# Loading 16 of 128 partitions of two experts' second weights in transfers of 8 partitions

## The chip, the cores and the metric

The kernel runs on one core of a Trainium2 chip. Five engines work side by side: PE (matrix products), DVE (vector work), ACT (scalar functions, copies out of PSUM), POOL and SP, which here mainly issue transfers. Sixteen DMA engines move data between HBM and SBUF, the on-chip memory of 128 partitions. Time is the device time of one execution in microseconds (us); the median of several executions counts.

## What is computed

Two stages follow each other. Attention over 8 batches, 8 heads, 576 positions and head size 64, in which heads 0 to 3 see the last 32 positions and heads 4 to 7 every fourth of the last 128; then a mixture of 8 experts with 4 slots each, on 4608 rows of width 512.

```python
def _attn_ref(q, k, v):                       # (8, 8, 576, 64) each
    scores = scale * np.matmul(q, k.transpose(0, 1, 3, 2))
    ...
    return np.matmul(attn, v)

def _moe_ref(x, phi, w1, w2):                 # x: (4608, 512), w1: (8, 512, 1024), w2: (8, 1024, 512)
    logits = x @ phi
    d = softmax of logits over the rows
    slot_input = d.T @ x                      # 32 slots, 4 for each expert
    for e in range(E):
        h = np.maximum(slot_input[e] @ w1[e], 0.0)
        slot_out[e] = h @ w2[e]
    c = softmax of logits over the slots
    return c @ slot_out
```

All inputs are float32 in HBM, and the output is float32. The weights of one expert are 2 MB (w1) and 2 MB (w2) there.

## The kernel before

**Loads.** All inputs but the first q and k come through POOL's queue, which is issued in the order in which the program is written. A load converts from float32 to float16 on its way, so a weight matrix of 2 MB becomes 1 MB in SBUF: 128 partitions with 4096 values each. Partition p of w2 holds the 8 rows 8p to 8p + 7 of the matrix side by side, which lie one after the other in HBM as well.

**Homes.** SBUF has eight large buffers, `home0` to `home7`. Batch b's raw q, k and v go to `homes[b]` (`load_batch`, L161). When the batch has been used up, expert b's weights take their place: w1 in the first half (`load_w1`, L237), w2 in the second (`load_w2`, L253). `load_w1(e)` and, for experts 0 to 4, `load_w2(e)` are issued within the attention loop (L638 to L641) after the work of batch e; w1 of expert 7 and w2 of experts 5, 6 and 7 follow the loop (L645 to L648). The w2 of expert 6 is loaded in a first half and two quarters, the w2 of expert 7 by left and right half of the columns and each half in two pieces, so that the left half of the result can be finished before the right one.

**Waits of the loads.** Loads on POOL's queue use eight semaphores in turn, so a load also waits until the one eight places ahead of it has landed. A load into a home waits in addition for the last reader of what was there.

**Order of the work.** In the attention loop over 32 units (two heads of one batch each) PE, ACT and DVE follow an order that a scheduler made. From L650 on ("tail") the order is written out by hand. There the slots' inputs are completed (`siT`, L689), then `expert_in(pr)` multiplies them by the w1 of two experts (L712), `expert_turn(pr)` transposes the result into `hTp` (L726 to L731), and `expert_out(e)` multiplies by w2 and adds up all experts in the PSUM tile `sop` (L741). For experts 6 and 7 this is split into the two halves of the columns (L793 to L798): for each half the rest of expert 6, expert 7, a copy of `sop` to `so` (by ACT for the left half, by DVE for the right one), and five output tiles. `finish_tile` (L770) multiplies by the softmax weights (`f`, L782), scales on ACT and DVE in turn (`ot`, L786 and L788) and issues the store on SP's queue (L791). Seven whole tiles follow. The last pieces of w2 that are loaded are those of the right half of expert 7 (L273).

The change touches `load_w2` and adds one constant next to `NV` (L40).

Of the kernel before, what the change touches and what calls it, by code (L numbers as in the profile page):

```python
# [37 lines left out]
OUT_COLS = [sum(nj for _, nj in OUT_TILES[:i]) for i in range(len(OUT_TILES))]  # L38
NU = 4 * B
NV = 2  # L40
SIDES = ((0, DMODEL // 2), (DMODEL // 2, DMODEL))
PIECES = ((0, 6), (6, 8))
HALF = 4
# [16 lines left out]
def kernel(  # L60
# [10 lines left out]
    nc = tc.nc  # L71
# [15 lines left out]
    for n, (nm, ten, by) in enumerate((("qp", q, nc.sync), ("kp", k, nc.scalar))):  # L87
        first[nm] = stage[0:NP, 768 * n : 768 * n + 768].rearrange("p (g x) -> p g x", g=2)
        by.dma_start(
            out=first[nm],  # L90
            in_=ten[0, 0:2].rearrange("h s d -> (h s) d").rearrange("(g p r) d -> p g (r d)", g=2, r=RP),
# [3 lines left out]
    def kept(shape, name, dt=FP16):  # L95
        return keep.tile(shape, dt, name=name, tag=name)
# [24 lines left out]
    ends = kept([128, 2, 130], "ends")  # L121
    vp = [kept([128, NKB + 1, 4, D + 1], f"vp{i}") for i in range(NV)]
    vd = [kept([128, 16, D + 1], f"vd{i}") for i in range(2)]
# [9 lines left out]
    for i in range(2):  # L133
        nc.vector.memset(vd[i][:, :, D : D + 1], 1.0)
    for i in range(NV):
        nc.vector.memset(vp[i][:, :, :, D : D + 1], 1.0)
# [72 lines left out]
    def select_v(b):  # L209
        raw, last = raws[b]["vp"], raws[b]["vt"]  # L210
        for i in range(2):
            sel = ps_s.tile([128, 2, 2, 4, D], FP32, name=f"sel{b}_{i}", tag="s")
            for r in range(4):
                for n in range(2):
# [8 lines left out]
                    )  # L223
            nc.scalar.copy(out=vp[b % NV][:, 2 * i : 2 * i + 2, :, 0:D], in_=sel[:, :, 0])
        end = ring.tile([128, 2, 4, D], FP32, name=f"sel{b}_2", tag="ring")
        for r in range(4):
# [7 lines left out]
            )  # L234
        nc.scalar.copy(out=vp[b % NV][:, 4:6, :, 0:D], in_=end)

# [9 lines left out]
    def load_half(e, side):  # L246
        d0, d1 = SIDES[side]
        nc.gpsimd.dma_start(
            out=w_tiles[e][1][:, HALF:8, d0:d1],
            in_=moe_w2[e].rearrange("(p c) f -> p c f", p=128)[:, HALF:8, d0:d1],  # L250
        )

    def load_w2(e):  # L253
        w2t = w_tiles[e][1]
        w2_from = moe_w2[e].rearrange("(p c) f -> p c f", p=128)
        if e == E_EXP - 2:
            nc.gpsimd.dma_start(
                out=w2t[:, 0:HALF].rearrange("p c f -> p (c f)"),
                in_=w2_from[:, 0:HALF].rearrange("p c f -> p (c f)"),
            )  # L260
            load_half(e, 0)
            return
        if e < E_EXP - 2:
            nc.gpsimd.dma_start(
                out=w2t.rearrange("p c f -> p (c f)"), in_=w2_from.rearrange("p c f -> p (c f)")
            )
            return
        w2t = w_tiles[e][1] = w2t.rearrange("p c f -> p (c f)").rearrange("p (s c f) -> p s c f", s=2, c=8)
        for n, (d0, d1) in enumerate(SIDES):
            if n == 1:  # L270
                load_half(e - 1, 1)
            for c0, c1 in PIECES:
                nc.gpsimd.dma_start(out=w2t[:, n, c0:c1], in_=w2_from[:, c0:c1, d0:d1])  # L273
# [148 lines left out]
    def values(u):  # L422
# [11 lines left out]
        for h in range(2):  # L434
            mms = []
            for blk in range(NKB):
                if plain:
                    mms.append((blk, Pp[:, h, blk, 0:128], vp[b % NV][:, blk, hl + h, :]))
                    if blk > 0:
                        mms.append((blk, Pp[:, h, blk - 1, 128:256], vp[b % NV][:, blk - 1, hl + h, :]))  # L440
                elif blk < 4:
# [100 lines left out]
    def front_slots(b, up=None):  # L542
# [3 lines left out]
        for n in range(9):  # L546
            j = n % 4
            d0, d1 = (0, DMODEL) if n == 8 else SIDES[n // 4]
            nc.tensor.matmul(  # L549
# [15 lines left out]
    def last_slots(last, dcs):  # L565
        er, x = Er[(B - 1) % 2], xs[B - 1]
        for dc in dcs:
            to = last[:, N_SLOTS * dc : N_SLOTS * dc + N_SLOTS]
            for blk in range(4):
                for g in range(2):  # L570
                    d0, d1 = SIDES[g]
                    nc.tensor.matmul(
# [42 lines left out]
    for u in range(NU - 2):  # L615
        st = scores(u + 1)
        if u + 3 < NU:
            regroup(u + 3)
        values(u)
        softmax_parts(u + 1, st)  # L620
        if u + 3 < NU:
            transposes(u + 3)
        b, ph = divmod(u - 4, 4)
        if b >= 0:
            if ph == 1:
                front_logits(b)
            elif ph == 2:
                front_rows(b)
            elif ph == 3:
                front_slots(b)  # L630
        if u == 1:
            spread_phi()
        if u >= 1:
            x_transposes(u - 1)
        if u % 4 == 3 and u // 4 + 1 < B:
            spread_v(u // 4 + 1)
            select_v(u // 4 + 1)
        if u % 4 == 2 and u // 4 < E_EXP - 1:  # L638
            load_w1(u // 4)
            if u // 4 < E_EXP - 3:  # L640
                load_w2(u // 4)  # L641
        if 26 <= u:
            nc.gpsimd.memset(hTp[u - 26], 0.0)

    load_w1(E_EXP - 1)  # L645
    load_w2(E_EXP - 3)
    load_w2(E_EXP - 2)
    load_w2(E_EXP - 1)  # L648

# [25 lines left out]
    for c in range(2):  # L675
# [14 lines left out]
        out=siT,  # L690
# [45 lines left out]
    def expert_out(e, side=None, chs=range(8)):  # L736
        d0, d1 = (0, DMODEL) if side is None else SIDES[side]
        w2t = w_tiles[e][1][:, side] if e == E_EXP - 1 else w_tiles[e][1][:, :, d0:d1]
        for ch in chs:
            j = ch % 4  # L740
            nc.tensor.matmul(  # L741
                sop[32 * j : 32 * j + 32, d0:d1],
                hTp[e % 4][:, ch, 28 - 4 * e : 60 - 4 * e],
                w2t[:, ch, :],
                start=(e == 0 and ch < 4),
                stop=(e == E_EXP - 1 and ch >= 4),
                skip_group_check=True,
            )
# [43 lines left out]

    for n, (d0, d1) in enumerate(SIDES):  # L793
        expert_out(E_EXP - 2, n, range(HALF, 8))
# [40 lines left out]
```

## Time and profile before

| | |
|---|---|
| median of 3 runs | 181.22 us (181.01 to 181.52) |
| the profiled execution | 181.12 us |
| its span, first to last instruction | 179.4 us |
| PE, DVE, ACT, POOL busy | 145.9, 124.1, 116.2, 52.9 us |
| mean granted clock of PE | 0.902 |
| HBM read, written | 62.02 MB, 9.44 MB |
| weight loads of 1 MB (as written to SBUF) | 14, 28.0 us from issue to landing in the median |

The profile is one execution. Its page gives the busy time of each engine, the span in 40 slices, the transfers by queue, the chain of work that ended last, and the costliest groups of instructions. The trace behind it gives every instruction and every packet that the DMA engines moved, with start, length and size. A line such as "L741" is a line of the kernel as printed above; "sop<-home,hTp" reads as written tile and read tiles. Queue q0 is POOL's, q1 SP's, q10 ACT's; q8 and q14 bring instructions.

### The profile page before, as it was taken

What the parts mean: (1) busy time and instruction counts of PE and PEld (TensorE: products, weight loads), DVE (VectorE), ACT (ScalarE), POOL (GpSimd) and SP (SyncE); (2) the same over time, 40 slices, a digit from 0 to 9 for tenths busy, and PEclk for the clock granted to TensorE, in tenths of its full rate; (3) what the DMA queues carried; (4) which work ended last, traced back from release to release, by engine and by line L of the source; (5) the groups of instructions that cost most, each with busy time, mean ns of one, the idle gap of its engine ahead of it and who ended that gap; (6) DMA issues with size and microseconds to landing.
All of it is one profiled execution on the core that took longest, in us unless ns stands there. A gap on an engine that the chain in (4) does not pass through costs nothing.

```text
span 179.4 us, 5142 instructions
## 1 busy us (share of the span) xinstructions
PE 145.9 (81%) x2138; PEld 98.0 (55%) x2138; DVE 124.1 (69%) x341; ACT 116.2 (65%) x216; POOL 52.9 (30%) x86
## 2 busy tenths in 40 slices
PE   6549988999989989989998998998888997797000
PEld 2324666777576667667666757765658343342000
DVE  7407699689799978978979979876862011799200
ACT  2236768687888789789789788877721131699100
POOL 7946545454554644401110005006111100000000
PEclk9975699579999999999999999999998599999755
DMA  5999999999999999999999999999999999999995
GB/s 154 193 199 202 202 203 201 201 203 202 203 202 201 202 201 204 219 221 210 212 225 212 216 219 212 217 216 210 223 214 214 212 194 192 264 384 422 433 425 227
DMA packets 29238, 41.11 MB, mean 229 GB/s; under 512 B 1696, under 2 KB 26400, under 8 KB 26784
## 3 DMA queue, kind: packets, MB, share of 16 engines
q0 software_dynamic: 24416, 30.68, 98.0%
q1 hardware_dynamic: 4592, 9.82, 14.1%
q10 hardware_dynamic: 208, 0.29, 0.6%
q8 instruction: 16, 0.26, 0.5%
q14 instruction: 6, 0.05, 0.1%
HBM read 62.02 MB, written 9.44 MB: 398 GB/s over the span
## 4 chain that ended last, share of the span: by engine, by line
PE 30%; DMA 28%; DVE 17%; ACT 9%; issue 5%; POOL 3%; DVEq 0%; ACTq 0%; POOLq 0%
DMA home<-in_moe_w_dram 24%; PE o L448 6%; DMA home<-in_v_dram 4%; PE rgx L468 4%; ACT qT L305 4%; DVE ot L788 4%; PE sel L227 3%; PE l L486 3%; ACT pr L369 3%; PE s L343 3%; DVE x L453 3%; DVE P L395 2%; PE f L782 2%; DVE kTd L320 2%; PE u L549 2%
## 5 line engine op out<-in xcount | busy, mean ns | idle before, releaser
L453 DVE TENSOR_TENSOR x<-o,rc 128x640 f16<-128x640 f32 x32 | 26.3, 821 | 0.4
L369 ACT ACTIVATE pr<-s 128x960 f16<-128x960 f32 (+1 forms) x32 | 22.9, 761 | 1.6 <-PE s L343 1.6
L376 ACT ACTIVATE pd<-s 128x640 f16<-128x640 f32 x32 | 22.0, 713 | 2.1 <-PE s L352 2.0
L171 POOL DMA_DIRECT2D home<-in_v_dram x24 | 16.6, 692 | 14.9 <-DMA home<-in_k_dram 8.8
L448 PE MATMUL o<-vd,P 128*128 128x65 f16 x256 | 14.5, 198 | 3.2 <-DVE x L453 2.6
L240 POOL DMA_DIRECT2D home<-in_moe_w_dram x8 | 4.2, 531 | 40.8 <-PE rgq L315 33.4
L474 ACT COPY xT<-rgx 128x512 f16<-128x512 f16 x16 | 9.4, 586 | 10.2 <-PE rgx L468 10.2
L448 PEld LDWEIGHTS <-P 128*128 128x128 f16 x288 | 12.2, 100 | 6.8 <-DVE x L453 3.6
L385 DVE TENSOR_TENSOR Pp<-pr,fixed 128x1280 f16<-128x1280 f16 (+1 forms) x32 | 15.4, 497 | 0.3 <-ACT pr L369 0.3
L448 PE MATMUL o<-vp,Pp 128*128 128x65 f16 x288 | 15.3, 201 | 0.0
L468 PE MATMUL rgx<-fixed,x 128*128 128x128 f16 x155 | 14.0, 222 | 1.3 <-DVE x L453 0.6
L448 PEld LDWEIGHTS <-Pp 128*128 128x128 f16 x288 | 12.0, 102 | 4.1 <-issue 2.4
L788 DVE TENSOR_SCALAR ot<-f,rrow 128x256 f32<-128x256 f32 (+1 forms) x24 | 12.8, 610 | 2.1 <-PE f L782 2.1
L305 ACT COPY qT<-rgq 128x576 f16<-128x576 f16 x16 | 10.2, 639 | 6.1 <-PE rgq L304 5.4
L395 DVE TENSOR_TENSOR P<-pd,fixed 128x1024 f16<-128x1024 f16 x16 | 10.8, 672 | 4.7 <-ACT pd L376 4.7
L468 PEld LDWEIGHTS <-x 128*128 128x128 f16 x160 | 10.1, 98 | 6.6 <-issue 4.2
L786 ACT ACTIVATE ot<-f,rrow 128x256 f32<-128x256 f32 (+1 forms) x24 | 11.9, 601 | 2.5 <-PE f L782 1.7
L320 ACT COPY qT<-rgq 128x576 f16<-128x576 f16 x16 | 10.2, 640 | 4.1 <-PE rgq L315 4.0
L782 PE MATMUL f<-so,ET 128*128 128x256 f16 (+1 forms) x48 | 10.7, 324 | 2.3 <-ACT ot L786 1.1
L320 DVE COPY kTd<-rgk 128x576 f16<-128x576 f16 x16 | 12.3, 772 | 0.0
L197 POOL DMA_DIRECT2D home<-in_k_dram x15 | 10.0, 667 | 7.8 <-DMA home<-in_q_dram 7.1
L315 PEld LDWEIGHTS <-home 96*128 96x128 f16 x192 | 10.4, 103 | 3.3 <-DMA home<-in_q_dram 2.0
(119 smaller groups left out, 319.4 us busy)
## 6 DMA issues: line engine op xcount, KB each, us to landing
home<-in_moe_w_dram POOLq DMA_DIRECT2D x14, 1024.0 KB, 28.0
out_dram<-ot SPq DMA_DIRECT2D x5, 1024.0 KB, 7.8
home<-in_q_dram POOLq DMA_DIRECT2D x15, 288.0 KB, 9.8
home<-in_k_dram POOLq DMA_DIRECT2D x15, 288.0 KB, 9.9
home<-in_v_dram POOLq DMA_DIRECT2D x16, 256.0 KB, 9.8
out_dram<-ot SPq DMA_DIRECT2D x8, 256.0 KB, 2.9
out_dram<-ot SPq DMA_DIRECT2D x4, 512.0 KB, 7.2
home<-in_moe_w_dram POOLq DMA_DIRECT2D x2, 384.0 KB, 22.5
```

Of the source, the lines that this page charges most:

```text
L171: nc.gpsimd.dma_start(out=dst, in_=v[b, h0 : h0 + n_h, r0 : r0 + 4 * n_p, :].rearrange("h (p r) d -> p h (r d)", r=4),)
L305: nc.scalar.copy(out=dst[:, 0:S].rearrange("c (p r) -> c p r", r=RP), in_=rg.rearrange("c r p -> c p r"),)
L320: (nc.scalar.copy if nm == "q" else nc.vector.tensor_copy)(out=dst[:, 0:S].rearrange("c (g p a) -> c g p a", g=4, a=3), in_=rg.rearrange(" ...
L369: nc.scalar.activation(out=(pr[:, :, 0 : 3 * QW], pr[:, :, 3 * QW :])[part], in_=st[:, :, 0 : (480, 224)[part]], func=AF.Exp, scale=SCALE,)
L376: nc.scalar.activation(out=pr[:, part].rearrange("p c e t -> p e c t"), in_=st[:, :, 0 : 2 * DW].rearrange("p e (c t) -> p e c t", c=2), f ...
L385: nc.vector.tensor_tensor(out=Pp[:, :, b0 : b0 + nb, 0:w], in0=pr[:, :, b0 * QW : b0 * QW + nb * w].rearrange("p h (t c) -> p h t c", c=w) ...
L395: nc.vector.tensor_tensor(out=P1.rearrange("p a c t -> p (a c) t"), in0=pr[:, :, :, 0:128].rearrange("p a c t -> p (a c) t"), in1=mask[:, ...
L448: nc.tensor.matmul(ot[:, h, blk], lhs, rhs, start=(n == 0), stop=(n == len(mms) - 1), skip_group_check=True)
L453: nc.vector.tensor_tensor(out=xs[b][:, :, 2 * D * hp : 2 * D * hp + 2 * D].rearrange("p t (h d) -> p h t d", h=2), in0=ot[:, :, :, 0:D], i ...
L468: nc.tensor.transpose(rg[:, 128 * blk : 128 * blk + 128], x[:, blk, hl : hl + 128], ident)
L782: nc.tensor.matmul(fp, ET[:, c0 : c0 + 127 * nj + 1 : nj], so[:, d0:d1], start=True, stop=True)
L788: nc.vector.tensor_scalar(out=ot[:, j], in0=fp, scalar1=scale, scalar2=None, op0=ALU.mult)
```

## The change

The w2 of experts 1 and 4 is no longer loaded in one transfer of 128 partitions with 4096 values each, but in four: partitions 0 to 111 whole, partitions 112 to 119 whole, then of partitions 120 to 127 the first 256 values, and then their other 3840. The other experts go through the same loop with one piece, as before.

```diff
 NV = 2
+UNEVEN = ((0, 112, 0, 4096), (112, 120, 0, 4096), (120, 128, 0, 256), (120, 128, 256, 4096))
 SIDES = ((0, DMODEL // 2), (DMODEL // 2, DMODEL))
...
         if e < E_EXP - 2:
-            nc.gpsimd.dma_start(
-                out=w2t.rearrange("p c f -> p (c f)"), in_=w2_from.rearrange("p c f -> p (c f)")
-            )
+            whole = w2t.rearrange("p c f -> p (c f)"), w2_from.rearrange("p c f -> p (c f)")
+            pieces = UNEVEN if e in (1, 4) else ((0, 128, 0, 4096),)
+            for p0, p1, x0, x1 in pieces:
+                to, of = (ap[p0:p1, x0:x1] for ap in whole)
+                nc.gpsimd.dma_start(out=to, in_=of)
             return
```

POOL issues six more transfers; no other engine's instructions change, and neither do the bytes.

## The prediction

> **What bounds the kernel now.** I read the page first. Its slices and queue rows say that the transfer engines never rest and that nearly all of their time belongs to one queue, POOL's loads (q0).
>
> ```profile
> DMA  5999999999999999999999999999999999999995
> ...
> q0 software_dynamic: 24416, 30.68, 98.0%
> q1 hardware_dynamic: 4592, 9.82, 14.1%
> q10 hardware_dynamic: 208, 0.29, 0.6%
> q8 instruction: 16, 0.26, 0.5%
> ```
>
> Next the chain that ended last, between 135 and 180 us (start, length, what). The reader is to see that its longest piece is the last weight load, and that everything from 155.24 on hangs on it.
>
> ```profile
> 140.13 15.06 DMA home<-in_moe_w_dram
> ...
> 155.24 0.30 PE sop L741 x2
> ...
> 155.63 0.43 DVE so L796
> ...
> 156.11 0.83 PE f L782 x6
> ```
>
> Then the timeline of PE at that place (start, length, engine, line, count, idle time before and who ended it). PE waits for weights only twice, at 154.56 and 155.24; `sop` of the left half, at 150.89, waited for DVE's `hTp` and not for a load.
>
> ```profile
> 150.89 0.73 PE L741 MATMUL sop<-home,hTp 128*32 128x512 f16 x16 [0.27 <-DVE hTp L731]
> 152.09 2.01 PE L782 MATMUL f<-so,ET 128*128 128x256 f16 x12 [0.48 <-ACT so L796]
> 154.03 0.29 PE L741 MATMUL sop<-home,hTp 128*32 128x256 f16 x4
> 154.56 0.40 PE L741 MATMUL sop<-home,hTp 128*32 128x256 f16 x6 [0.24 <-DMA home<-in_moe_w_dram]
> 155.24 0.29 PE L741 MATMUL sop<-home,hTp 128*32 128x256 f16 x2 [0.28 <-DMA home<-in_moe_w_dram]
> ```
>
> So there is little to gain and all to lose: without any wait for weights `sop` would start at 154.03 and its 0.29 + 0.40 + 0.29 us would end at 155.01 in place of 155.53. Earlier weights are worth at most 0.5 us; later ones cost the whole delay.
>
> Last, stretches of time (length, busy time and count of PE, PEld, DVE, ACT, POOL, the granted clock, DMA share, GB/s):
>
> ```profile
> 100.00:125.00 25.00, 22.91 (x391) 16.22 (x389) 20.63 (x54) 20.51 (x37) 4.87 (x10) 1.00 1.03 216
> ...
> 152.00:152.50 0.50, 0.41 (x4) 0.38 (x4) 0.00 (x0) 0.14 (x2) 0.00 (x0) 1.00 1.15 155
> 152.50:153.00 0.50, 0.48 (x5) 0.28 (x4) 0.49 (x2) 0.50 (x2) 0.00 (x0) 1.00 1.00 135
> 153.00:154.00 1.00, 1.00 (x6) 0.47 (x5) 1.00 (x3) 1.00 (x4) 0.00 (x0) 1.00 0.79 106
> ```
>
> The rate falls from 216 to 135 GB/s before the last load has landed: some of the 16 engines have run dry while others still carry weights. The trace's packet records (start, length, bytes of each) show which. Followed from packet to packet they fall into 16 unbroken chains, one an engine; I call them lanes. In a 1 MB weight load each lane moves 8 rows of 8192 bytes, one every 606 ns, and one completion packet of 22 ns: 8 x 606 + 22 = 4870 ns, which is the step from one landing to the next (120.4, 125.3, 130.1 us). The last load's sixteen completions come at 152.3, 152.4, 152.4, 152.6, 152.9, 153.2, 153.5, 154.0, 154.4, 154.6, 154.7, 154.8, 154.8, 154.9, 155.0 and 155.2 us. The kernel waits for the sixteenth. What splits the lanes is q8 above: 16 packets of 16 KB of instructions between 20.0 and 148.6 us, 893 to 974 ns each, whose lengths repeat after eight, and each of which makes one chain late. Eight lanes take two of them each (lags at the end 2.1 to 2.9 us behind the first lane), eight take none (0, 0, 0, 0.3, 0.5, 0.8, 1.1 and 1.7). I call them late and early lanes.
>
> **The change part by part.** Loads and bytes other than the w2 of experts 1 and 4 stay. Each of these two becomes 112 partitions, then 8, then 8 x 256 columns, then 8 x 3840 columns.
>
> *POOL.* Six more issues, by the six rows of L264 (528 to 541 ns) 6 x 0.53 = 3.2 us of POOL, which has 52.9 us of work in 179.4. A load waits for the landing of the load eight places ahead of it: the three issues at the end of this row follow the landings of w1 of experts 5, 6 and 7 (130.1, 135.0, 139.8 us).
>
> ```profile
> 123.52 0.55 POOL L257 DMA_DIRECT2D home<-in_moe_w_dram  x1
> ...
> 130.44 0.77 POOL L248 DMA_DIRECT2D home<-in_moe_w_dram  x1 [3.91 <-DMA home<-in_moe_w_dram]
> 135.26 0.82 POOL L273 DMA_DIRECT2D home<-in_moe_w_dram  x1 [4.05 <-DMA home<-in_moe_w_dram]
> 140.13 0.70 POOL L273 DMA_DIRECT2D home<-in_moe_w_dram  x1 [4.04 <-DMA home<-in_moe_w_dram]
> ```
>
> With more, smaller loads in that window of eight, some issues move: w1 of expert 2 from 72.03 to 75.5, w1 of expert 6 from 107.80 to 110.7, and behind it on POOL the memsets of `hTp` (L643; DVE needs them at 143.9). The first half of w2 of expert 6 moves from 123.52 to about 125. The last three wait for the same loads as before. Each time 15 to 25 us of other loads are still ahead in q0, so I cost all of it at nothing; that cover would be gone only if fewer than about one load's 4.9 us were queued.
>
> *The lanes.* 112 partitions are 7 rows a lane. A transfer of 8 partitions has 8 rows for 16 lanes, and no row of this trace shows where they go. The nearest are the 16-partition loads of v's last rows, where each lane gets the 8 packets of one partition: a partition stays in one lane. By that, eight lanes get a whole row and eight get none. The bounds:
> - All three small transfers, both times, on the same eight lanes. Heavy lanes then take per expert 8 x 606, the last row in two parts (41 ns a 512-byte packet, by the pitch in the loads of L273, and 606 x 3840/4096 = 568), and 4 x 22 for completions: 5545 ns, against 4870: +0.675. Light lanes: 7 x 606 + 88 = 4330: -0.54. For both experts +1.35 and -1.08 us.
> - The other half in the second expert, or the rows dealt over all lanes: 0.675 - 0.54 = +0.135 us on every lane.
>
> I take the first, since nothing in the trace shows a transfer's lanes to depend on the transfers before it, and keep the second for the range. Which lanes are heavy matters as much: the eight can avoid the late ones in only one way, by being exactly the early eight. Any other choice puts extra rows on a late lane. With the latest lane among them the last landing goes from 155.2 to 155.2 + 1.35 = 156.55.
>
> *Behind it.* The left half's last piece, which landed at 151.2, comes at 152.55; its two matmuls and the copy (0.30 + 0.42, by the same steps of the right half) delay the first f from 152.09 to about 153.4, and its 2.01 us end at 155.4, ahead of the last landing. `sop` then ends at 156.88, and DVE's `so` and everything behind it shift by 1.35. The output does not take it back: of its 17 transfers the large ones land 2.43 us apart (165.9, 168.4, 170.8 us), as fast as they go. Span 179.4 + 1.35 = 180.75. The profiled execution took 181.12, its span plus 1.72 around it, and the median of the runs is 181.22: 182.47 by the one, 182.57 by the other. I say **182.5**.
>
> The Trainium skill (page "DMA: Bandwidth & Descriptors", section "Why a DMA increments its semaphore by 16 and not by 1") says that a transfer goes to as many engines as divide its outermost counts, here eight, and that on this path a cursor moves on from one such transfer to the next. By that rule two large pieces with a small one between them share a half, three transfers flip the halves for the second expert, and the sum is the +0.135 of the second bound. The same section has an exception, measured on trn2, for some direct copies: equal shares from the first engine on, which is the first bound. No row here tells the two apart.
>
> **The rivals.**
> - *Turn about.* Each expert loads another half. For it: a transfer of 8 rows leaves half the lanes out, and dealing to the lanes in turn would even that out over six transfers. Against it: in no row of this trace does a lane's share depend on what was loaded before. Every lane +0.135: 181.35, within 0.3%.
> - *The heavy lanes are the early ones* (the other side, not slower). Late lanes end at 2.9 - 1.08 = 1.8; the latest early lane at 1.7 + 1.35 = 3.05, 0.15 later than the latest now: 181.4. It decides from the extra load at which that one lane passes 2.9, 1.2 us. Without that lane (its 1.7 contains a single 8 KB instruction packet of q14 at 129.3 us) the next ends at 1.1 + 1.35 = 2.45, the weights land 0.45 earlier, and the limit of 0.5 us above allows that: 180.8, and 180.6 to 180.7 if the right half uses all of the limit.
> - *The pieces are dealt over all 16 lanes after all*, the change doing nothing: +0.135, 181.35.
>
> **How the numbers follow.** Same eight lanes, late ones among them: 0.65. Turn about 0.15. Early lanes 0.15, of which 0.08 for a gain and 0.07 for the lane at 1.7. Dealt over all 0.05. About 0.3%, 0.54 us, is what a measurement of this kernel can tell from no change. Faster is 0.08; same 0.15 + 0.07 + 0.05 = 0.27; slower 0.65. The likeliest case alone spans 182.0 (the latest lane is a light one and a lane at 2.4 the heavy one: 2.4 + 1.35 - 2.9 = +0.85) to 182.9. The range reaches from 181.0, so that the two cases at 181.35 are in it, to 183.0.
>
> **What would show it.** The last landing of the weights at 156.5 in place of 155.2, PE's last wait before `sop` about as much later and longer, and the GB/s of the stretch before it lower for longer. In the packet records: heavy chains with nine rows in both experts, and whether these are the chains with q8 packets. The prediction is wrong if the heavy chains change between the two experts, if they are the early ones, or if the last landing moves and the end does not.

## The result and the profile after

| | before | after |
|---|---|---|
| median, 7 runs each | 181.22 us (181.01 to 181.77) | 182.80 us (182.34 to 184.44) |
| ratio, 95% interval | | 1.0086 [1.0062, 1.011] |
| the profiled execution, its span | 181.12, 179.4 us | 182.80, 180.7 us |
| first matmul of the expert part (`h`) | 139.68 us | 139.24 us |
| last landing of the weights | 155.2 us | 156.6 us |

A second comparison of the same two kernels, told below, gave 1.0046 [1.0024, 1.0067]. By the one the change costs about 1.6 us, by the other 0.8. Ratios here and below leave out executions in a slow state, of which the second comparison had one among its 12 (187.62 us).

The packet rows first: the kernel before, then the changed one. POOL's queue has 160 packets more than before (24576), of which 16 come from the rows that are cut in two (in each of the two experts 8 rows of 8192 bytes became 8 packets of 512 and 8 of 7680). The other 144 are 4-byte packets: six more transfers with sixteen completions each are 96, and 48 are left over. That is eight for each of six small transfers: a transfer of 8 partitions leaves eight lanes without a row, and each of these gets an empty packet. That excludes the rival in which the pieces are dealt over all 16 lanes.

```profile
DMA packets 29238, 41.11 MB, mean 229 GB/s; under 512 B 1696, under 2 KB 26400, under 8 KB 26784
```

```profile
DMA packets 29398, 41.11 MB, mean 228 GB/s; under 512 B 1840, under 2 KB 26560, under 8 KB 26960
...
q0 software_dynamic: 24576, 30.68, 97.4%
```

The chain that ended last (start, length, what), as before through the last load. That load lands 1.38 us later, at 156.57.

```profile
141.49 15.08 DMA home<-in_moe_w_dram
...
156.61 0.41 PE sop L744 x2
...
157.11 0.44 DVE so L799
```

PE's timeline at that place (start, length, engine, line, count, idle time before and who ended it). Before, no load held up the left half; here its two last steps wait for loads (0.79 and 0.27 us), its first `f` starts at 153.33 in place of 152.09, and the right half's `sop` takes from 155.47 to 157.0. The last row merges twelve matmuls with the short waits between them.

```profile
150.61 0.51 PE L744 MATMUL sop<-home,hTp 128*32 128x512 f16 x8 [0.27 <-DVE hTp L734]
151.91 0.40 PE L744 MATMUL sop<-home,hTp 128*32 128x256 f16 x6 [0.79 <-DMA home<-in_moe_w_dram]
152.58 0.29 PE L744 MATMUL sop<-home,hTp 128*32 128x256 f16 x2 [0.27 <-DMA home<-in_moe_w_dram]
153.33 2.21 PE L785 MATMUL f<-so,ET 128*128 128x256 f16 x12 [0.46 <-ACT so L799]
155.47 1.54 PE L744 MATMUL sop<-home,hTp 128*32 128x256 f16 x12
```

Stretches of time in the changed kernel (length, busy time and count of PE, PEld, DVE, ACT, POOL, granted clock, DMA share, GB/s). From 154 to 155 only 35 GB/s move, where the kernel before already had 259 with its first stores: most lanes are empty and few still carry weights. And the granted clock falls from 1.00 to 0.50 there. Before, it stayed at 1.00. The row of the kernel before, then three of the changed one:

```profile
154.00:155.00 1.00, 0.72 (x11) 0.23 (x11) 0.95 (x3) 0.69 (x2) 0.00 (x0) 1.00 0.94 259
```

```profile
153.00:154.00 1.00, 0.67 (x6) 0.59 (x6) 0.25 (x1) 0.64 (x2) 0.00 (x0) 1.00 0.87 116
154.00:155.00 1.00, 0.98 (x7) 0.57 (x5) 1.00 (x4) 1.00 (x4) 0.00 (x0) 0.71 0.26 35
155.00:156.00 1.00, 0.94 (x11) 0.25 (x12) 1.00 (x4) 0.94 (x3) 0.00 (x0) 0.50 0.52 155
```

The sixteen completions of the last load say it best. Before they came at 152.3, 152.4, 152.4, 152.6, 152.9, 153.2, 153.5, 154.0, 154.4, 154.6, 154.7, 154.8, 154.8, 154.9, 155.0 and 155.2; now at

151.5, 152.1, 153.7, 153.7, 153.7, 153.8, 153.8, 153.8, 154.0, 154.1, 154.2, 154.2, 154.3, 155.2, 155.9 and 156.6.

The first comes 0.8 earlier, the last 1.4 later, and the spread grew from 2.9 to 5.1 us. The same bytes are spread worse.

POOL's issues (the same columns as for PE) went about where the prediction had them: w1 of experts 2 and 6 at 76.06 and 110.80, the first half of w2 of expert 6 at 125.63, and the last load (141.49 in the chain above) still 15 us ahead of its landing.

```profile
76.06 0.56 POOL L241 DMA_DIRECT2D home<-in_moe_w_dram  x1 [0.79 <-PE s L355]
...
110.80 0.54 POOL L241 DMA_DIRECT2D home<-in_moe_w_dram  x1 [4.29 <-PE s L355]
...
125.63 0.53 POOL L258 DMA_DIRECT2D home<-in_moe_w_dram  x1 [2.46 <-DMA home<-in_moe_w_dram]
```

### The profile page after: what moved, and what is told of

The parts are those of the page before. It is cut to its first block, busy times and chain, and to the rows that moved or that the text cites. A ratio compares the mean times of both kernels' runs of the same rounds, so it can differ in the third digit from the quotient of the medians.

```text
span 180.7 us, 5152 instructions
## 1 busy us (share of the span) xinstructions
PE 147.2 (81%) x2138; PEld 98.1 (54%) x2138; DVE 125.7 (70%) x341; ACT 116.9 (65%) x216; POOL 56.9 (31%) x92
## 3 DMA queue, kind: packets, MB, share of 16 engines
q0 software_dynamic: 24576, 30.68, 97.4%
## 4 chain that ended last, share of the span: by engine, by line
PE 27%; DMA 27%; DVE 22%; ACT 9%; issue 6%; POOL 3%; DVEq 0%; ACTq 0%; POOLq 0%
DMA home<-in_moe_w_dram 22%; PE o L451 6%; DMA home<-in_v_dram 4%; DVE ot L791 4%; DVE x L456 4%; PE rgx L471 4%; ACT qT L308 4%; PE l L489 3%; ACT pr L372 3%; DVE P L398 3%; PE sel L228 3%; PE s L346 2%; DVE kTd L323 2%; PE f L785 2%; DVE P L406 2%
## 5 line engine op out<-in xcount | busy, mean ns | idle before, releaser
L789 ACT ACTIVATE ot<-f,rrow 128x256 f32<-128x256 f32 (+1 forms) x24 | 12.4, 585 | 3.1 <-PE f L785 2.3
L785 PE MATMUL f<-so,ET 128*128 128x256 f16 (+1 forms) x48 | 11.8, 386 | 2.3 <-ACT ot L789 1.1
L225 ACT CAST vp<-sel 128x512 f16<-128x512 f32 x16 | 9.5, 596 | 3.9 <-PE sel L217 3.9
```

The costliest lines, as they stand in the source:

```text
L785: nc.tensor.matmul(fp, ET[:, c0 : c0 + 127 * nj + 1 : nj], so[:, d0:d1], start=True, stop=True)
```

## The experiments

The theory: a transfer of 8 partitions always falls on the same eight lanes, the lanes that it leaves out catch nothing up for the others, and late lanes are among the heavy ones. Its rivals: the set of eight lanes changes from transfer to transfer; the small transfer between two large ones shifts it; or the cost is in the splitting itself (POOL's issues, a load of 112 partitions, the completions). Diffs are against the changed kernel. "Completions" are those of the last load of the weights. Each group was measured beside the kernel before on one chip: at a median of 181.47 for it in the first eight experiments, and at 181.34 to 181.74 in the others. A diff shows the lines that differ, and "..." stands for lines left out. Where an expectation places the last landing, 155.2 of the kernel before is what it counts from.

### Without the small transfer

```diff
-UNEVEN = ((0, 112, 0, 4096), (112, 120, 0, 4096), (120, 128, 0, 256), (120, 128, 256, 4096))
+UNEVEN = ((0, 112, 0, 4096), (112, 120, 0, 4096), (120, 128, 0, 4096))
```

> Experts 1 and 4 in three transfers each: 112 partitions, 8, 8, all of whole rows; the small transfer between the two large ones is gone. Same eight lanes every time: a heavy lane takes 9 x 606 + 3 x 22 = 5520 ns in place of 4870, +0.65 us per expert, so the last landing of the weights goes from 155.2 to about 156.5 and the time up by 1.3 us, ratio 1.007. Turn about: the two transfers of 8 fall on one half each, every lane has 8 rows again, +0.09 us in all, ratio 1.000 to 1.001. If the number of transfers as such were the cost, four extra in place of six give two thirds of what the change cost, about +1.0 us.

Measured: 182.19 us, ratio 1.0037 [1.0018, 1.0056]; last completion 156.2, first 151.2, spread 5.0. So the small transfer isn't what does it: if two transfers of 8 partitions took turns, every lane would have eight rows and the spread would be 2.9. The time is up by about half of what was expected (1.007). The time alone would also fit a cost of each transfer as such; the next kernel tells the two apart. The trace has 96 more 4-byte packets than before, 64 completions and 4 x 8 empty ones.

### The sixteen partitions in one transfer

```diff
+UNEVEN = ((0, 112, 0, 4096), (112, 128, 0, 4096))
```

> Experts 1 and 4 in two transfers each: 112 partitions and 16. Every lane gets 7 rows and 1, so both theories on lanes say nothing but two more completion packets of 22 ns, +0.04 us: ratio 1.000, last landing at 155.2, and no extra packets in the trace other than 32 completions. If splitting w2, or the rate of a transfer of 112 partitions, or POOL's waits on transfers eight places back were the cost, a third of the change's cost or more should remain, +0.5 us.

Measured: 181.56 us, ratio 0.9996 [0.9979, 1.0013]; last completion 155.6, spread 3.0, and 32 more small packets, all completions. The experts are split here as well, but each lane gets its eighth row, and the cost is gone. Neither the splitting nor 112 partitions cost anything that can be measured: a third of the change's cost would be 1.003 by the first comparison and 1.0015 by the second, and the interval ends at 1.0013.

### Expert 1 alone

```diff
-            pieces = UNEVEN if e in (1, 4) else ((0, 128, 0, 4096),)
+            pieces = UNEVEN if e in (1,) else ((0, 128, 0, 4096),)
```

> The change on expert 1 alone. Same eight lanes: +0.675 us on the heavy ones, last landing 155.9, ratio 1.0035 to 1.004, each execution alike. Turn about: three transfers leave the other half to the next execution, so that the executions take turns between the lanes that hold the latest one (+0.675) and those that do not, and the times should fall into two groups.

Measured: 181.55 us, ratio 1.0001 [0.9982, 1.0019]; completions from 151.8 to 155.4, spread 3.6. This went against the expectation: half the change should have cost half of it. The heavy lane that ended last came only 0.2 later than before. The mechanism allows it if the latest heavy lane isn't the latest of all: one that lags 2.4 in place of 2.9 ends at 2.4 + 0.675 - 2.9 = +0.2. That it lagged by so much here is not shown. The times don't fall into two groups either, as turn about would have it: ten of the twelve lie between 181.24 and 181.85. PE's timeline shows that the left half again waits for no load, and the right half as in the kernel before:

```profile
152.47 2.01 PE L785 MATMUL f<-so,ET 128*128 128x256 f16 x12 [0.47 <-ACT so L799]
154.41 0.70 PE L744 MATMUL sop<-home,hTp 128*32 128x256 f16 x10
155.41 0.28 PE L744 MATMUL sop<-home,hTp 128*32 128x256 f16 x2 [0.31 <-DMA home<-in_moe_w_dram]
```

### Transfers of 8 partitions by halves of the columns

```diff
-            for p0, p1, x0, x1 in pieces:
...
+            nc.gpsimd.dma_start(out=whole[0][0:112], in_=whole[1][0:112])
+            for p0 in (112, 120):
+                for d0, d1 in SIDES:
+                    nc.gpsimd.dma_start(out=w2t[p0 : p0 + 8, :, d0:d1], in_=w2_from[p0 : p0 + 8, :, d0:d1])
```

> Experts 1 and 4 in five transfers each: 112 partitions, and then for partitions 112 to 119 and 120 to 127 the left and the right 256 of each 512 columns, so that a partition of such a transfer is 8 packets of 512 bytes. Same eight lanes: 7 x 606 + 32 x 41 + 5 x 22 = 5664 ns, +0.79 us per expert, last landing about 156.8, ratio 1.008. Turn about: two of the four on each half, 7 x 606 + 16 x 41 + 5 x 22 = 5008 ns, +0.14 us per expert, last landing about 155.5, ratio 1.0015. By the section of the Trainium skill's page 'DMA: Bandwidth & Descriptors' on why a DMA increments its semaphore by 16, its exception is for some direct copies only; a transfer whose rows are in pieces may follow the cursor even if whole rows do not. Then this kernel is near 1.0015 while the one without the small transfer is near 1.007.

Measured: 181.99 us, ratio 1.0026 [1.0008, 1.0044]; completions from 152.7 to 155.8 and one at 156.7. A partition now is eight separate runs of 512 bytes, and the result is another: taken in order of time, all completions but the last moved by 0.1 to 0.8, and the spread without the last one is 3.1. Even dealing costs per expert 7 rows (4242 ns), two partitions of 8 packets (2 x 328), twice eight empty packets of 6 ns, and five completions: 4242 + 656 + 96 + 110 = 5104, 0.23 more than 4870; +0.47 for both. The records show the turns: one lane carries eight 512-byte packets from 121.64 us on, eight empty ones from 121.99, eight of 512 bytes from 122.04 and eight empty ones from 122.39. Transfers whose partitions are several runs do take turns. The empty packets follow the runs: 640 more small packets, 128 completions and 512 empty, which is eight for each of eight lanes in each of eight transfers.

The one lane at 156.7 stays unexplained.

### The change, measured again

No edit; the same kernel beside the kernel before in another session, with more runs.

> The change itself once more, beside the others and on their chip. Same eight lanes, two or three of the late ones among them: last landing near 156.5, first near 151.3, ratio 1.007. If the first comparison's 1.0086 belonged to its chip or its day, the ratio here is nearer to the 1.0037 of the kernel without the small transfer.

Measured: 182.44 us (12 runs), ratio 1.0046 [1.0024, 1.0067]; completions 151.3, 152.0, then 153.6 to 154.5, and 155.4, 155.9, 155.9. The same pattern with the last lane 0.7 us earlier than in the first profile, and the first `h` at 137.90. `sop` ends at 156.36, 0.66 us ahead of the first profile, just as far as the last landings lie apart (155.91 and 156.57).

### Four experts

```diff
+            pieces = UNEVEN if e in (1, 2, 3, 4) else ((0, 128, 0, 4096),)
```

> The change on experts 1, 2, 3 and 4: twice the extra rows. Same eight lanes: heavy 4 x 0.675 = +2.7 us, light 4 x -0.5 = -2.0, so the sixteen last completions spread over some 7 us and the last is at 157.9; ratio 1.014 to 1.015. If something that happens once were the cost (a wait of POOL, one late transfer), the ratio stays at that of the change.

Measured: 183.87 us, ratio 1.0145 [1.01, 1.019]; completions from 150.2 to 157.3, spread 7.1. Each further expert drives the two groups of lanes further apart, by 7.1 - 2.9 = 4.2 in four experts; by the prediction's terms it would be 4 x (0.675 + 0.54) = 4.9 if the first lane were light and the last one heavy. Turn about can't give this. The chain goes through the last load as in the changed kernel:

```profile
142.25 15.08 DMA home<-in_moe_w_dram
...
157.37 0.41 PE sop L744 x2
```

### Turns of unequal size

```diff
-            for p0, p1, x0, x1 in pieces:
...
+            nc.gpsimd.dma_start(out=whole[0][0:112], in_=whole[1][0:112])
+            for p0 in (112, 120):
+                for d0, d1 in ((0, 32), (32, 512)):
+                    nc.gpsimd.dma_start(out=w2t[p0 : p0 + 8, :, d0:d1], in_=w2_from[p0 : p0 + 8, :, d0:d1])
```

If transfers of several runs take turns, small, large, small, large puts both large ones on the other eight lanes.

> Experts 1 and 4 in five transfers: 112 partitions, then for partitions 112 to 119 and for 120 to 127 the first 32 and the other 480 of each 512 columns, 8 packets of 64 and of 960 bytes a partition. In the kernel with left and right halves such transfers took turns between the two sets of eight lanes. If they do, the small ones go to one set and the large ones to the other: heavy 7 x 606 + 16 x 72 + 16 x 6 + 5 x 22 = 5600 ns, +0.73 us per expert, +1.46 in all, the others about -0.2 each. If the large ones fall on the set that the whole-row transfers leave out, the lanes that are late because of q8 are mostly in it: five or six completions close together at 155.5 to 156.5, the last near 156.4, ratio 1.006 to 1.008. If they fall on the same set as the whole rows, two or three completions at the end as in the change. If they do not take turns, small and large fall on one set, heavy +0.85 us per expert, and the last is near 156.9.

Measured: 183.34 us, ratio 1.0105 [1.0071, 1.0139], more than the 1.006 to 1.008 expected (the wait for the left half, told at the end, adds to it); completions 151.6, 151.7, 151.7, 152.4, 152.4, 153.1, 153.8, 153.8, 153.8, 154.1, and after a gap of two us 156.1, 156.3, 156.4, 156.4, 156.7, 156.8. Six lanes end in a bunch: the eight lanes that the large transfers fell on hold six late ones. In the changed kernel only three lanes end beyond 154.3, at 155.2, 155.9 and 156.6: two late ones, and the early one of 154.0 with its +1.35. So whole rows fall on the other eight, which hold two late lanes and six early ones.

### Looking for the two

Three kernels give the lanes of expert 1 unequal shares, in whole rows; in these, and in the staircase behind them, expert 4 is loaded whole. If such transfers are dealt from the first lane on, the number of rows of a lane is given by its place. The records don't number the lanes, so the places below go by this rule.

```diff
+UNEVEN = ((0, 96, 0, 4096), (96, 112, 0, 4096), (112, 118, 0, 4096), (118, 124, 0, 4096), (124, 128, 0, 4096))
```

> Expert 1 alone, in transfers of whole rows of 96, 16, 6, 6 and 4 partitions. By the rule that whole rows are dealt one a lane from the first lane on, lanes 0 to 5 get 9 or 10 rows, the ten others 7 (-0.5 us). If the first six lanes are early ones, the late lanes end 0.5 us sooner and the last landing moves from 155.2 to 154.7 or stays, if the early lane at 1.6 is among the four with 10 rows (+1.3): ratio 0.997 to 1.000. If late lanes are among the first six, the last landing is at 155.9 to 156.5, ratio 1.004 to 1.007.

Measured: 181.83 us, ratio 1.0023 [1.0004, 1.0043]; three completions before 152.3, the last two 155.4 and 155.9. By the rule the first four lanes have ten rows, the next two nine, the others seven.

```diff
+UNEVEN = ((0, 112, 0, 4096), (112, 120, 0, 4096), (120, 124, 0, 4096), (124, 126, 0, 4096), (126, 128, 0, 4096))
```

> Expert 1 alone, in transfers of whole rows of 112, 8, 4, 2 and 2 partitions. Dealt from the first lane on, lanes 0 and 1 get 11 rows, 2 and 3 get 9, 4 to 7 get 8, the upper eight 7: shifts of +1.9, +0.7, +0.1 and -0.5 us. With a late lane (2.2 to 2.9 at the end) among the first two, the last landing is at 156.5 to 157.1; with late lanes only from lane 2 on, at 155.2 to 155.9; with early lanes alone among the first four, it stays at 155.2 to 155.3, or at 155.9 if the early lane at 1.6 is one of the first two.

Measured, one run: 181.44 us beside 181.34; completions from 152.4 to 155.3. By the rule the first two lanes have eleven rows, the next two nine, the next four eight, the others seven.

```diff
+UNEVEN = ((0, 112, 0, 4096),) + tuple((p, p + 4, 0, 4096) for p in range(112, 128, 4))
...
+            pieces = UNEVEN if e in (1,) else ((0, 128, 0, 4096),)
```

> Expert 1's second half of w2 is loaded as 112 partitions and four transfers of 4 partitions each, whole rows; expert 4 as before. Theory (transfers whose partition is one run are dealt from the first lane on, and the late lanes are not among the first four): lanes 1 to 4 get eleven rows and lanes 5 to 16 seven. Eleven rows and five completions are 11 x 606 + 5 x 22 = 6776 ns, +1.9 us; seven rows with five completions and four empty packets are about 4.4 us, -0.45 us. The late lanes then end at 154.7 to 154.8; if all of the first four are early (0.6 us or less behind the first) the last landing is 154.7 to 154.9 and the ratio 0.997 to 0.999. If the early lane at 1.6 us is among the first four, or one of the late ones, the last landing is 155.4 to 155.9 or beyond 156.8 and the ratio 1.000 to 1.003 or more. Rival (the set of lanes that a transfer falls on changes from one to the next, so that the sixteen partitions are dealt evenly): nine to eight rows everywhere, last landing within 0.2 us of the kernel before, ratio 0.999 to 1.001.

Measured: 182.23 us beside 181.74 (10 and 15 runs), ratio 1.0034 [1.0018, 1.0049]; completions 151.8, 151.9, 151.9, 152.2, then eleven from 153.8 to 154.9, and the last at 155.8. (What is split is the whole w2 of expert 1, not its second half.) The good case did not come. One lane that had not been late was made the last: 155.8 less the 1.9 that eleven rows cost is 153.9, near the 154.0 of the early lane with the 8 KB instruction packet. No late lane is among the first four: the earliest of them, at 154.4, would have ended at 156.3. The late lanes end at 154.9 or earlier, 0.3 ahead of the kernel before, where seven rows promised 0.45. An even deal (no lane changed) is excluded. Even so the ratio is at the upper edge of what a last landing at 155.8 gives, and PE's timeline shows a reason that isn't the last landing: the left half's first `f` takes 2.72 us in place of 2.01.

```profile
151.10 0.40 PE L744 MATMUL sop<-home,hTp 128*32 128x256 f16 x6 [1.48 <-DMA home<-in_moe_w_dram]
...
152.64 2.72 PE L785 MATMUL f<-so,ET 128*128 128x256 f16 x12 [0.46 <-ACT so L799]
155.29 0.91 PE L744 MATMUL sop<-home,hTp 128*32 128x256 f16 x12
```

Taken together, and if the lags of the lanes are the same from one execution to the next (which they are only roughly), the two late lanes of the lower eight are among lanes 5 to 8, one of them 5 or 6 (ten and nine rows sent a lane to 155.9, and eight rows none beyond 155.3). This is argued from three profiles, not shown lane by lane.

### Expert 1 in a staircase of sixteen transfers

```diff
+COUNTS = tuple(range(15, 0, -1)) + (8,)
+UNEVEN = tuple((sum(COUNTS[:i]), sum(COUNTS[: i + 1]), 0, 4096) for i in range(len(COUNTS)))
```

> Expert 1's w2 in sixteen transfers of whole rows, of 15, 14, 13 and so on down to 1 partitions, and of 8 at the end. It asks which lanes are late. If whole rows are dealt one a lane from the first lane on, whatever went before, lane 0 gets 16 rows, lane 1 15, down to lane 7 with 9, lane 8 7 and lane 15 none, so that every lane is known by the rows it takes, and the q8 packets in it can be counted. The chains then move apart by steps of 606 ns over some 9.7 us, the last landing of the weights is at 157.5 (lane 0 early) to 160 (late), and the time is up by 2.5 to 5 us. If transfers took turns between lanes, each one starting where the last one ended, the lanes would stay within some 2 us of one another and the last landing near 156.

Measured, one run: 186.27 us beside 181.53; last landing 160.1. It was meant to mark each lane by its count of rows and failed at that: the small loads filled the eight places in flight, POOL's next load waited for the landing eight places back, and the queue ran dry. All lanes stood level again afterwards, so no mark could be read. POOL's timeline shows the waits (first row) and the burst that came too late (last row).

```profile
91.84 0.50 POOL L270 DMA_DIRECT2D home<-in_moe_w_dram  x1 [5.78 <-DMA home<-in_moe_w_dram]
...
93.28 3.60 POOL L270 DMA_DIRECT2D home<-in_moe_w_dram  x7 [0.19 <-issue]
```

It is of use for another reason: it shows what the prediction's "cover" is worth. Where less than one load is queued ahead, the six cheap issues of this change would not be cheap. The load ahead of the sixteen transfers has its first completion at 88.4, and the first seven of them have theirs at 88.6, 88.8 and so on up to 89.6, never more than 0.24 us apart, while a row takes 0.61. So one lane got no row in any of the seven, not even in the one of 15 partitions. A deal that moved on from where the last one ended would have reached it.

### One load less

```diff
     def load_w2(e):
+        if e == 3:
+            w_tiles[3][1] = w_tiles[2][1]
+            return
         w2t = w_tiles[e][1]
```

This is the kernel before without the load of expert 3's w2; its product is taken with the w2 of expert 2, so expert 3's own second weights have no part in the output. It asks what earlier weights are worth.

> The kernel before without the load of expert 3's w2; its place in the product is taken by the w2 of expert 2, so 1 MB less goes through the queue and the output leaves out expert 3's own weights. The last landing of the weights moves from 155.2 to 150.3. If earlier weights are worth at most 0.5 us, because the order of PE and the copies holds the right half of sop until 154.03, the time falls by 0.5 us, ratio 0.997. If the loads as such set the time, it falls by the load's 4.9 us, ratio 0.973.

Measured: 179.80 us beside 181.34, ratio 0.9902 [0.9885, 0.9919]; that is -1.5 us by the medians and -1.8 by the ratio; last landing 150.8. PE waits for no load at the end:

```profile
150.04 0.73 PE L744 MATMUL sop<-home,hTp 128*32 128x512 f16 x16 [0.27 <-DVE hTp L734]
151.24 2.01 PE L785 MATMUL f<-so,ET 128*128 128x256 f16 x12 [0.47 <-ACT so L799]
153.18 0.51 PE L744 MATMUL sop<-home,hTp 128*32 128x256 f16 x12
```

`sop` ends at 153.7, 1.8 us ahead of the 155.53 of the kernel before, where the prediction had a limit of 0.5. Of this, 0.85 us is an earlier start (153.18 in place of 154.03). The rest is the right half itself: its twelve matmuls take 0.51 us in one go, and took 1.50 with two waits.

## Why the prediction was right, point by point

**What binds.** Right: the last landing sets the end in both kernels, in the second profile of the change as well, and from there on everything shifts. The large stores again land 2.4 to 2.5 us apart (169.7, 172.1, 174.6) and take nothing back.

**POOL at nothing.** Right. Three issue times were forecast at 75.5, 110.7 and about 125 us, and came at 76.06, 110.80 and 125.63. The kernel with sixteen partitions in one transfer (1.000) bounds what splitting alone costs. The staircase shows that the condition attached to it was real.

**The same eight lanes.** Right, as the likeliest case had it. The packet records of the changed kernel show it lane by lane, which the prediction had named as a test. Only a lane that gets a row of the cut part carries one of its 512-byte packets. They start at 92.89, 92.96, 93.09, 93.36, 93.58, 93.96, 94.04 and 94.64 us for expert 1, and at 122.76, 122.83, 123.23, 123.27, 123.45, 123.83, 124.99 and 125.62 for expert 4. Five of the eight come again after 29.87 us. The other three (93.09, 94.04 and 94.64) come 0.32, 1.09 and 1.11 us later than that. This fits one instruction packet in between, of 8 KB for the first (0.32 us) and of 16 KB for the other two (0.9 to 1.1 us). The lanes without a row show in one burst the empty packets of all three small transfers; five of these eight bursts come again after 28.63 us, the others later. So the heavy lanes of expert 1 are those of expert 4. Partitions 112 to 119 and 120 to 127 fall on the same lanes, so their place in SBUF does not decide it.

The other runs agree from several sides: no turns (the kernel without the small transfer), eight empty packets for each small transfer, and a spread that grows with the number of experts (2.9 us for none, 3.6 for one, 5.1 and 4.6 for two, 7.1 for four). The Trainium skill, page "DMA: Bandwidth & Descriptors", section "Why a DMA increments its semaphore by 16 and not by 1", has a rule (a cursor that moves on) and an exception (some direct copies take equal shares from the first engine on). Both agree with runs here, for different loads: whole rows, one run a partition, follow the exception as far as the same lanes go (that they are the first ones, no record shows); partitions of several runs take turns, as the rule says (1.0026 by halves, 1.0105 with unequal turns).

**Which lanes are heavy.** "With the latest lane among them the last landing goes from 155.2 to 155.2 + 1.35 = 156.55" came out at 156.6 in the first profile, but this is the step whose size is least certain, and that it was met so closely is in part luck. The heavy set holds two late lanes and six early ones: the two whose 512-byte packets came 1.09 and 1.11 us late are the last to end, 30.9 us on, at 155.9 and 156.6. The prediction asked only that one late lane be heavy, which all choices but one give; that the latest of all was one of two among eight it could not know. And how late the later of the two is differs from one execution to the next. Taking the extra off the last landing gives the lane's lag by itself: 156.6 - 1.35 = 155.25 in the first profile, 155.9 - 1.35 = 154.55 in the second, 155.4 - 0.675 = 154.7 with expert 1 alone, 157.3 - 4 x 0.675 = 154.6 with four. Three of four lie 0.5 to 0.7 below the latest of the kernel before. That is the low case that the prediction named for its own range ("a lane at 2.4 the heavy one"). So +0.7 to +0.85 is as typical as +1.35, and the two ratios, 1.0086 and 1.0046, lie on either side of the 1.0071 that 182.5 makes of 181.22. Between the two profiles the last landing accounts for the whole difference; what made the medians of the two comparisons differ is not settled.

**Heavy and light lanes.** The two intervals of 29.87 and 28.63 us hold five whole loads, 24.35 us at 4.87 each. That leaves 5.52 us for a heavy lane and 4.28 for a light one, where 5.545 and 4.33 were forecast. In the completions -0.54 an expert was right as well: the first completion went from 152.3 to 151.8 with one expert and to 150.2 with four, -0.5 and -0.53 an expert. With two it came at 151.5 and 151.3, where 151.2 was to be expected.

**Behind the landing.** The left half's last piece was forecast at 152.55 and landed at 152.5; the first `f` at about 153.4 began at 153.33; `f` was to end at 155.4 and ended at 155.54. `sop` was to end at 156.88 and ended at 157.02, since its last two matmuls took 0.41 in place of 0.30 us at half the clock. Span 180.75 against 180.7.

**Where it failed.** "Earlier weights are worth at most 0.5 us." Taking one load away made `sop` end 1.8 us earlier, and the time fell by 1.5 to 1.8. Two terms of that limit were wrong. It added the right half's three groups, 0.29 + 0.40 + 0.29 us, each with a start of its own; in one go the twelve matmuls take 0.51. Even from 154.03 on, `sop` would have ended near 154.54, and the limit would have been 1.0 us. And it took the start of PE's last work (154.03) from one profile as if it were fixed. The first `h` began at 139.68 there, but at 139.24 in the changed kernel, and between 137.79 and 139.68 in the other profiles of this study, with kernels whose work before it is the same but for the loads. The profiled execution was one of the latest. It follows that in an earlier one PE reaches the left half while its last piece is still to land, so that the weights bind more; no second profile of the kernel before was taken to show it. The rival for a gain (the early lanes heavy) was therefore priced too low; it didn't come about, so the forecast was not hurt. In place of the fixed start belongs a range, which one profile can't give. Why the start varies was not looked into.

## What to carry to other kernels

A load that the kernel waits for as a whole is as late as its latest lane, so count rows per lane and not bytes: here a transfer of 8 partitions with one run each put its rows on the same lanes every time, and two such transfers didn't even each other out. Keep the count at a multiple of sixteen, or check in the packet records that transfers take turns. And before a limit on a gain is read from slack in one profile, ask how firmly the start of the work on the other side of it is known, and how long that work takes when nothing interrupts it.

## What the runs showed beyond that

**A wait on PE costs twice.** In the profiles where PE waits 0.79 us or more for the left half's last piece, its granted clock falls to 0.50 within a few us and the work behind it takes longer. This is read from the profiles; no run changed the wait alone. The rows from 150 to 154 us of the kernel without the small transfer (columns as above):

```profile
150.00:151.00 1.00, 0.00 (x0) 0.00 (x0) 0.00 (x0) 0.00 (x0) 0.00 (x0) 1.00 1.44 193
...
152.00:153.00 1.00, 0.34 (x3) 0.24 (x3) 0.00 (x0) 0.37 (x1) 0.00 (x0) 0.73 1.28 173
153.00:154.00 1.00, 1.00 (x6) 0.67 (x6) 0.43 (x2) 0.65 (x2) 0.00 (x0) 0.50 0.82 110
```

| kernel | first `h` | wait for the left half's load | clock at 154.5 to 155 us | twelve `f` of the left half |
|---|---|---|---|---|
| before | 139.68 | none | 1.00 | 2.01 us |
| expert 1 alone | 139.64 | none | 1.00 | 2.01 |
| one load less | 138.75 | none | 1.00 | 2.01 |
| the three groups (8, 4, 2 and 2 partitions) | 138.24 | 0.29 | 1.00 | 2.00 |
| changed | 139.24 | 0.79 | 0.50 | 2.21 |
| sixteen partitions in one | 138.52 | 0.98 | 0.50 | 2.42 |
| first four lanes | 138.73 | 1.48 | 0.50 | 2.72 |
| without the small transfer | 138.20 | 1.68 | 0.50 | 2.71 |

The other profiles with a wait fit in: 1.16 and 1.29 us with 2.21 and 2.38 us of `f` (the change again, four experts), 1.67 to 1.69 with 2.65 to 2.72 (halves, unequal turns, shares of 96 to 4 partitions, staircase).

The wait of 1.5 us and more costs 0.7 us again in `f`, which delays the right half's `sop`: with the first four lanes heavy the chain of waits no longer goes through the last load, but through the left half's last piece and its `f`. The same holds for the kernel without the small transfer, the two with turns and the staircase, so their times are not set by the last landing alone.

```profile
125.81 25.94 DMA home<-in_moe_w_dram
...
152.64 2.72 PE f L785 x12
155.36 0.85 PE sop L744 x12
```

The Trainium skill, page "TensorE: Matmul & The Clock Gate", Part 1, has two states, half and full, and a fall to half after an idle window of about 3.4 us. The rows agree with the two values; but PE was not idle for that long anywhere here: in the changed kernel its matrix products took 1.9 of the 3.4 us up to the fall at about 154.4, and its longest pause there was 0.79 us.

**Empty packets.** A lane that gets no row of a transfer still gets a 4-byte packet for each run that a partition has, besides its completion. In such a burst they follow each other by 6 ns: the four completions and three empty packets of a light lane in the changed kernel pass in 0.06 us.
